# Running sums of attention weights moved half a visit later in the last two batches

## The chip, the cores and the metric

The kernel runs on one core of a Trainium2 chip. The metric is the device time of one execution in microseconds. The median of three runs of the kernel before is 1086.68 us (1086.46 to 1087.05).

## The reference, cut to what matters

Attention with hashed buckets, over 4 batches, 8 heads, 768 positions and 64 features, followed by a mixing block with a Fourier transform and a two-layer network on 512 channels:

```python
q_bucket = np.sum((q @ proj > 0) * powers, axis=-1)      # 6 bits; k_bucket alike
mask = q_bucket[:, :, :, None] == k_bucket[:, :, None, :]
scores = np.where(mask, scale * q @ k.T, -1e9)
attn = softmax(scores)                                   # numerator / (sum over keys + 1e-9)
x = (attn @ v) laid out as (B, S, H*D)

mixed = np.real(fft(fft(x, axis=1), axis=2))
u = x + mixed
un = (u - mean(u)) / sqrt(var(u) + 1e-6)
out = u + relu(un @ w_ch1) @ w_ch2
```

For this document the denominator matters: the sum over all keys of the masked exponentials. The kernel adds up the masked weights of the six chunks of keys in a tile `acc`, and sums over partitions only once for each pair of heads.

## The kernel before, in words

Work is done batch by batch. Attention of batch b runs beside the mixing block of batch b-1, which is a Python generator called `other`; between two steps of the attention generator, two or three steps of `other` are taken. For the first batch the order of instructions on each engine is as written. For the others a planner orders each engine's queue: an instruction goes out when its data and buffers are ready in the planner's own account of time, the earliest written first; scores and values (`behind`) are given precedence over what was written up to 500 instructions earlier. The order is fixed before the kernel runs, and each engine takes its queue in that order.

Attention handles a pair of heads n (n = 4b + t, four pairs in a batch) and six chunks c of 128 keys. For one chunk TensorE multiplies scores `sc` (L905) for both heads and both halves of the queries, ScalarE writes their exponentials into one of two buffers `pk` (L916), VectorE masks these in place, one instruction for each head (L930), TensorE multiplies with v into `oo` (L941), and VectorE adds the chunk's weights to `acc` (L1018, 128 partitions x 1536 elements). The first two chunks' weights are added straight out of the two buffers, so there are five sums in a pair. After the last chunk, `scale` sums `acc` over partitions with TensorE (`sum`, L960), and VectorE and ScalarE make the reciprocals (L967 to L981) and multiply x by them. `acc` has one buffer: the first sum of a pair comes after the `sum` matmuls of the pair before.

In the first two batches (n < 8) a visit handles one chunk. In the last two (n >= 8, batches 2 and 3 of 0 to 3) a visit with even c handles two chunks: scores, values of the chunk two before, exponentials, masks and sum of c, then the same of c+1. The visit with odd c does no attention work but takes a step of `prepare` (transposes L779 and hash bits of the next pair) or of `fold` (the first step of the mixing block), and then `other` goes on.

`other`, the mixing block, has four stages: matmuls `cs` (L1133); matmuls `A` and `B` (L1162), whose results VectorE adds into x (L1176); the hidden layer's products `h_p` (L1441), which ScalarE copies out of PSUM (L1463 to L1492) and VectorE combines (L1467, L1474, L1479, L1483, L1491); and the outer products `o` (L1320), which VectorE adds to the result (L1332). Hidden layer and outer products come twice in a batch. A and B, `h_p`, `o`, `sum` and the bits use one PSUM pool of two banks, so that a product can only start when VectorE or ScalarE has emptied a bank. SP issues the loads of q, k and v as well as the fetches of weights `w` (L1414, L1325).

`done_by` remembers the newest instruction on ScalarE and on VectorE of certain kinds: exponentials, masks (L930), additions into x (L1176), and most of the hidden layer's copies and additions. `in_turn()` queues what is written inside it behind these, each on its own engine. That is an order alone; it waits for no completion.

Of the kernel before, what the change touches and what calls it, by code (L numbers as in the profile page):

```python
# [485 lines left out]
def _main(  # L486
# [27 lines left out]
    def wt(shape, dtype, tag, name, bufs=2):  # L514
        return work.tile(shape, dtype, tag=tag, name=name, bufs=bufs)
# [95 lines left out]
    for i in range(NPK):  # L611
        pk = const.tile([P, 2, 2, HALF + 1], F32, tag=f"pk{i}", name=f"pk{i}")
# [70 lines left out]
    @contextmanager  # L683
    def in_turn():

        with ExitStack() as st:
            for ins in done_by.values():
                st.enter_context(tc.issue_after(ins.ins))
            yield
# [186 lines left out]
    @contextmanager  # L876
    def behind():

        with tc.issue_after(last[0].ins), tc.high_priority(offset=AHEAD):
            yield  # L880
# [3 lines left out]
    def scores(n, c, glued=False):  # L884

        qt, kt, qb, kb = preps[n]
        pss = []
        ks = slice(c * P, (c + 1) * P)
        heads = [slice(h * D, (h + 1) * D) for h in range(2)]
        for g in range(2):  # L890
            qs = slice(g * HALF, (g + 1) * HALF)
            ps = ps_sc.tile([P, 2, 512], F32, tag="sc", name=f"sc{n}_{g}_{c}")
            if kb is None:

                at = (c + (NT // 2 if g else 0)) % NT * P
                for h, rows in enumerate(heads):
                    nc.tensor.matmul(
                        ps[:, h, 0:HALF], qb[rows, 1, at : at + P],
                        qb[rows, 0, g * HALF : (g + 1) * HALF],
                        start=True, stop=False,  # L900
                    )

            for h, rows in enumerate(heads):
                with behind() if (g + h or glued) and n >= NPAIR else nullcontext():
                    last[0] = nc.tensor.matmul(  # L905
                        ps[:, h, 0:HALF], kt[rows, ks], qt[rows, qs],
                        start=kb is not None, stop=True,
                    )
            if n < TWO:
                weights(pks[npk[0] % NPK], g, ps)  # L910
            pss.append(ps)
        return pss

    def weights(pk, g, ps):

        done_by[ET.Activation] = nc.scalar.activation(  # L916
            pk[:, g, :, 0:HALF], ps[:, :, 0:HALF], AF.Exp, scale=SCALE
        )

    def weigh(n, c, pss):  # L920

        qb, kb = preps[n][2:]
        pk = pks[npk[0] % NPK]
        npk[0] += 1
        for g in range(2) if n >= TWO else ():
            weights(pk, g, pss[g])
        if kb is not None:
            for h in range(2):
                w = pk[:, :, h, 0:HALF]
                done_by[ET.DVE] = nc.vector.scalar_tensor_tensor(  # L930
                    w, qb[:, h].rearrange("p (g s) -> p g s", g=2), kb[:, h, c : c + 1], w,
                    op0=ALU.is_equal, op1=ALU.mult,
                )
        return pk

    def values(n, c, pk, oos):

        for g in range(2):
            w = HALF + 1 - g
            for h in range(2):  # L940
                oo = nc.tensor.matmul(  # L941
                    oos[g][h * D : (h + 1) * D, 0:w], nat["v", n][:, (2 * c + h) * D : (2 * c + h + 1) * D],
                    pk[:, g, h, 0:w], start=(c == 0), stop=(c == NT - 1),
                )
        last[0] = oo

    def scale(n, oos, sums):


        x = xs[n // NPAIR][:, n % NPAIR]  # L950
        vs = wt([P, 1], F32, "vs", f"vs{n}")
        nc.scalar.copy(vs, oos[0][:, HALF : HALF + 1])
        halves = [x[:, g * HALF : (g + 1) * HALF] for g in range(2)]
        for g, xg in enumerate(halves):
            nc.scalar.activation(xg, oos[g][:, 0:HALF], AF.Identity, bias=vs)

        ps = pt([P, HALF], f"sum{n}")
        for i, part in enumerate(sums):
            for j in range(4):
                nc.tensor.matmul(  # L960
                    ps[32 * j : 32 * j + 32, :], ones, part[:, j // 2, j % 2],
                    start=(i == 0), stop=(i == len(sums) - 1),
                )


        rt = wt([P, S], F32, "rt", f"rt{n}", 1)
        nc.vector.transpose(rt[:, 0:HALF], ps)  # L967
        rc = wt([P, HALF // 32], F32, "rc", f"rc{n}")
        nc.vector.tensor_scalar(rc, rt[:, 0:HALF:32], S * EPS, None, op0=ALU.add)
        nc.vector.reciprocal(rc, rc)  # L970
        yield
        rr = wt([P, 2, HALF // 32], F32, "rr", f"rr{n}")
        for g in range(2):
            for i in range(4):
                j = 2 * g + i // 2
                nc.scalar.copy(rr[32 * i : 32 * i + 32, g], rc[32 * j : 32 * j + 32])  # L976
        nc.vector.transpose(
            rt.rearrange("p (j i) -> p j i", i=32),
            rr.rearrange("p g j -> p (g j)")[:, :, None].broadcast_to([P, S // 32, 32]),
        )  # L980
        nc.vector.tensor_tensor(x, x, rt, op=ALU.mult)  # L981

    def attention(b):
        xs[b] = wt([P, NPAIR, S], F32, "x", f"x{b}")
        pending, scales = [], []

        def finish():
            n, c, pk, oos, sums = pending.pop(0)
            with behind() if n >= NPAIR and t is not None else nullcontext():
                values(n, c, pk, oos)  # L990
            if c == NT - 1:
                scales.append(scale(n, oos, sums))
                next(scales[-1])

        for t in range(NPAIR):
            n = NPAIR * b + t
            half = fold(b, 0) if t == NPAIR - 1 else iter(())
            if 1 < n + 1 < NPAIR * B:
                load(n + 1)
            ahead = prepare(n + 1) if n + 1 < NPAIR * B else iter(())  # L1000
            oos = [ps_o.tile([P, 512], F32, tag="o", name=f"oo{n}_{g}") for g in range(2)]
            acc = wt([P, 2, 2, HALF], F32, "acc", f"acc{n}", 1)
            first = None
            def chunk(c, pss):

                nonlocal first
                pk = weigh(n, c, pss)
                new = pk[:, :, :, 0:HALF]
                sums = [acc]
                if c == 0:  # L1010
                    first = new
                elif c == NT - 1 and b == 0:

                    sums.append(new)
                else:

                    for g in (0, 1) if b == 0 else (slice(0, 2),):
                        nc.vector.tensor_tensor(  # L1018
                            acc[:, g], (first if c == 1 else acc)[:, g], new[:, g],
                            op=ALU.add,  # L1020
                        )
                return n, c, pk, oos, sums

            for c in range(NT):
                if n < TWO:
                    new = chunk(c, scores(n, c))

                    for sc in scales:
                        next(sc, None)
                    scales.clear()  # L1030
                    while pending:
                        finish()
                    for sc in scales if b else ():
                        next(sc, None)
                    pending.append(new)
                elif c % 2 == 0:
                    pss = scores(n, c)
                    if len(pending) > 1:
                        finish()
                    new = [chunk(c, pss)]  # L1040
                    if pending:
                        finish()
                    new.append(chunk(c + 1, scores(n, c + 1, True)))
                    for sc in scales:
                        next(sc, None)
                    scales.clear()
                    pending += new
                if c > (3 if b == 1 else 2):
                    next(half, None)
                if c > 0:  # L1050
                    next(ahead, None)
                yield
        t = None
        while pending:
            finish()
        for sc in scales:
            next(sc, None)
# [586 lines left out]
```

## Time and profile before

| | |
|---|---|
| median of three runs | 1086.68 us |
| the profiled execution | 1086.83 us |
| its span, first to last instruction | 1085.0 us |
| TensorE busy | 1034.9 us, 95% |
| VectorE busy | 789.9 us, 73% |
| ScalarE busy | 498.4 us, 46% |
| running sums L1018, all batches | 92 instructions |
| masks L930 | 132 instructions, 128.9 us |
| granted TensorE clock | 0.995 |

Busy time is the time in which an engine executes. PE is TensorE, DVE VectorE, ACT ScalarE, SP the engine that issues most DMAs. In a line of the timeline stand the start in us from the beginning of the span, the time taken, the engine and line of code, the operation with what it writes and reads, how many were merged, and, in brackets, how long the engine had been idle before and what ended that. A line of the waits names who waited for whom, the us in total, how often, and the longest.

### The profile page before, as it was taken

The page shows a single profiled execution, that of the slowest core. Times are in us where ns is not written, and L with a number is a line of the kernel's source. Part 1 is how long each engine was busy: PE and PEld are TensorE (multiplying, and loading weights), DVE is VectorE, ACT ScalarE, POOL GpSimd, SP SyncE. Part 2 cuts the span into 40 slices and gives each one's busy share as a digit, 9 for nine tenths or more (in the row PEclk, how much of TensorE's full clock was granted, in tenths as well). Part 3 has the DMA queues.
Part 4 walks back from the last instruction along what each step waited for, and adds up shares of the span by engine and source line. Part 5 has one row for each costly group of instructions (what it writes and reads, how often), then busy time and mean ns, then how long its engine had stood idle before and what let it go on. Part 6 is the DMA issues. An engine that isn't in the chain of part 4 may idle for free.

```text
span 1085.0 us, 14130 instructions
## 1 busy us (share of the span) xinstructions
PE 1034.9 (95%) x4933; PEld 633.1 (58%) x4933; DVE 789.9 (73%) x1336; ACT 498.4 (46%) x1055; POOL 58.3 (5%) x132
## 2 busy tenths in 40 slices
PE   7989898999999999999999999999999999999997
PEld 3333364547644675545664576645675579768676
DVE  5899969887699978685948776876865875644353
ACT  6988554762277233545335424354315522340430
POOL 0000000002000020010000020001000002100000
PEclk9999999999999999999999999999999999999999
DMA  8663452380056260223062233213033205122401
GB/s 214 190 142 76 97 144 54 121 243 1 22 133 229 71 205 15 59 68 83 11 190 72 60 97 126 44 44 91 17 100 100 73 20 175 58 80 85 129 20 42
DMA packets 175710, 103.13 MB, mean 95 GB/s; under 512 B 129552, under 2 KB 162960, under 8 KB 175632
## 3 DMA queue, kind: packets, MB, share of 16 engines
q1 hardware_dynamic: 169840, 88.65, 30.3%
q0 software_dynamic: 4224, 13.11, 3.9%
q8 instruction: 41, 0.67, 0.3%
q10 hardware_dynamic: 1568, 0.39, 0.2%
q14 instruction: 37, 0.30, 0.1%
HBM read 81.14 MB, written 20.97 MB: 94 GB/s over the span
## 4 chain that ended last, share of the span: by engine, by line
PE 64%; DVE 24%; ACT 6%; issue 3%; SPq 1%; DMA 1%; DVEq 0%; ACTq 0%
PE o L1320 24%; PE h_p L1441 19%; PE oo L941 7%; PE sc L905 6%; DVE pk L930 5%; DVE acc L1018 5%; PE cs L1133 2%; PE A L1162 1%; ACT pk L916 1%; ACT rr L976 1%; PE B L1162 1%; DMA kn<-in_k_dram 1%; SPq L576 1%; DVE w L643 1%; DVE qt L779 1%
## 5 line engine op out<-in xcount | busy, mean ns | idle before, releaser
L1320 PE MATMUL o<-w,h 128*128 128x256 f32 x1152 | 258.8, 381 | 2.4 <-ACT tq L1339 0.9
L1320 PEld LDWEIGHTS o<-w,h 128*128 128x128 f32 x1152 | 216.7, 190 | 42.9 <-issue 4.3
L916 ACT ACTIVATE pk<-sc 128x768 f32<-128x768 f32 x192 | 147.3, 808 | 98.2 <-PE sc L905 32.9
L1441 PE MATMUL h_p<-x,w 128*128 128x384 f32 x448 | 162.3, 492 | 0.1
L905 PE MATMUL sc<-qt,kt 64*128 64x384 f32 x768 | 154.8, 506 | 3.6 <-ACT pk L916 3.3
L930 DVE SCALAR_TENSOR_TENSOR pk<-qb,kb,pk 128x768 f32<-128x768 bf16 x132 | 128.9, 1011 | 33.4 <-ACT pk L916 33.1
L941 PE MATMUL oo<-pk,vn 128*64 128x385 f32 (+1 forms) x768 | 148.1, 497 | 4.0 <-DVE pk L930 3.4
L1441 PEld LDWEIGHTS h_p<-x,w 128*128 128x128 f32 x448 | 82.6, 190 | 64.2 <-issue 7.7
L1018 DVE TENSOR_TENSOR acc<-acc,pk 128x1536 f32<-128x1536 f32 (+1 forms) x72 | 105.8, 1484 | 5.8 <-ACT pk L916 5.1
L1441 PE MATMUL h_p<-w 128*128 128x384 f32 x288 | 106.4, 492 | 3.5 <-ACT w L1478 2.3
L941 PEld LDWEIGHTS oo<-pk,vn 128*64 128x64 f32 x768 | 50.8, 136 | 91.6 <-issue 74.2
L905 PEld LDWEIGHTS sc<-qt,kt 64*128 64x128 f32 x768 | 66.9, 188 | 55.0 <-issue 19.3
L1441 PEld LDWEIGHTS h_p<-w 128*128 128x128 f32 x288 | 53.0, 190 | 45.5 <-ACT w L1490 5.1
L1332 DVE SCALAR_TENSOR_TENSOR w<-o,rs,w 128x256 f32<-128x256 f32 x56 | 26.7, 479 | 42.6 <-PE o L1320 42.6
L1350 ACT COPY tq<-o 128x256 f32<-128x256 f32 x24 | 8.9, 372 | 102.6 <-PE o L1320 102.6
L1320 PE MATMUL o<-w 128*128 128x256 f32 x176 | 42.1, 382 | 1.0 <-DVE w L1332 1.0
L1474 DVE TENSOR_TENSOR h<-h 128x384 f32<-128x384 f32 x32 | 17.7, 553 | 30.3 <-ACT h L1473 30.3
L1320 PEld LDWEIGHTS o<-w 128*128 128x128 f32 x176 | 33.0, 190 | 7.7 <-DVE w L1332 2.0
L1467 DVE TENSOR_TENSOR h<-h 128x384 f32<-128x384 f32 x32 | 17.7, 553 | 26.6 <-ACT h L1466 26.6
L1071 POOL DMA_DIRECT2D out_dram<-w x30 | 16.4, 548 | 368.1 <-ACT tq L1350 146.2
L1366 DVE TENSOR_TENSOR tq<-tq,o 128x256 f32<-128x256 f32 x24 | 10.0, 418 | 35.0 <-PE o L1320 35.0
L1339 ACT COPY tq<-o 128x256 f32<-128x256 f32 x24 | 8.8, 368 | 54.0 <-PE o L1320 53.9
(170 smaller groups left out, 1332.9 us busy)
## 6 DMA issues: line engine op xcount, KB each, us to landing
w<-ad SPq DMA_DIRECT2D x168, 128.0 KB, 2.0
w<-bd SPq DMA_DIRECT2D x42, 512.0 KB, 4.5
zraw<-in_moe_w_ch_dram POOLq DMA_DIRECT2D x16, 512.0 KB, 4.2
bd<-w SPq DMA_DIRECT2D x14, 512.0 KB, 3.6
vn<-in_v_dram SPq DMA_DIRECT2D x32, 192.0 KB, 3.5
qn<-in_q_dram SPq DMA_DIRECT2D x120, 48.0 KB, 2.4
kn<-in_k_dram SPq DMA_DIRECT2D x60, 96.0 KB, 3.1
zraw<-in_moe_w_ch_dram SPq DMA_DIRECT2D x8, 512.0 KB, 6.8
```

The lines of the kernel that those rows point to most:

```text
L905: last[0] = nc.tensor.matmul(ps[:, h, 0:HALF], kt[rows, ks], qt[rows, qs], start=kb is not None, stop=True,)
L916: done_by[ET.Activation] = nc.scalar.activation(pk[:, g, :, 0:HALF], ps[:, :, 0:HALF], AF.Exp, scale=SCALE)
L930: done_by[ET.DVE] = nc.vector.scalar_tensor_tensor(w, qb[:, h].rearrange("p (g s) -> p g s", g=2), kb[:, h, c : c + 1], w, op0=ALU.is_equa ...
L941: oo = nc.tensor.matmul(oos[g][h * D : (h + 1) * D, 0:w], nat["v", n][:, (2 * c + h) * D : (2 * c + h + 1) * D], pk[:, g, h, 0:w], start=( ...
L1018: nc.vector.tensor_tensor(acc[:, g], (first if c == 1 else acc)[:, g], new[:, g], op=ALU.add,)
L1133: nc.tensor.matmul(ps[:, pc + 2 * lo : pc + 2 * hi - 1 : 2], z[:, cp, pc, par, t * P : (t + 1) * P], ch[:, cp, pc, lo:hi], start=(cp == 0) ...
L1162: nc.tensor.matmul(ps[:, cols], F[:, par, k, t, j * P : (j + 1) * P], sq[:, t, k, cols], start=(t == 0), stop=(t == 1),)
L1320: nc.tensor.matmul(ps, a[:, r], right7[i][:, r], start=start and r == 0, stop=r == HF // 2 - 1, skip_group_check=not start,)
L1332: nc.vector.scalar_tensor_tensor(t[:, cols], src, r, t[:, cols], op0=ALU.mult, op1=ALU.add)
L1441: nc.tensor.matmul(ps, left[:, k], right[i][:, k], start=start and k == 0, stop=k == 1, skip_group_check=not start,)
L1467: done_by[ET.DVE] = nc.vector.tensor_tensor(c21, c12, c21, op=ALU.add)
L1474: done_by[ET.DVE] = nc.vector.tensor_tensor(c22, c21, c22, op=ALU.add)
```

## The change

In the two-chunk batches the running sums of both chunks of a visit are no longer written directly behind each chunk's masks, but in the following visit with odd c, which so far did nothing in `attention` but its steps of `fold` and `prepare`. They are written inside `in_turn()`, and so are queued on VectorE behind the newest instruction in `done_by`: a mask, an addition into x, or an addition of the hidden layer. `chunk` keeps scores' exponentials and masks; the sums are a function `tally` of their own. In the one-chunk batches `tally` follows `chunk` at once, as before.

```diff
             def chunk(c, pss):
 
+                return n, c, weigh(n, c, pss), oos, [acc]
+
+            def tally(c, pk, sums):
+
                 nonlocal first
-                pk = weigh(n, c, pss)
                 new = pk[:, :, :, 0:HALF]
-                sums = [acc]
                 if c == 0:
                     first = new
                 elif c == NT - 1 and b == 0:
...
                             acc[:, g], (first if c == 1 else acc)[:, g], new[:, g],
                             op=ALU.add,
                         )
-                return n, c, pk, oos, sums
 
             for c in range(NT):
                 if n < TWO:
                     new = chunk(c, scores(n, c))
+                    tally(c, new[2], new[4])
...
                     pending += new
+                else:
+                    with in_turn():
+                        for p in pending:
+                            tally(p[1], p[2], p[4])
                 if c > (3 if b == 1 else 2):
                     next(half, None)
```

## Prediction

> **What bounds the kernel now.** I read the page's first parts, then the waits of TensorE in the stretch of each of the last two batches of attention, and then the timeline of VectorE where the longest of those waits lies. The page:
>
> ```profile
> span 1085.0 us, 14130 instructions
> PE 1034.9 (95%) x4933; PEld 633.1 (58%) x4933; DVE 789.9 (73%) x1336; ACT 498.4 (46%) x1055; POOL 58.3 (5%) x132
> PEclk9999999999999999999999999999999999999999
> L1018 DVE TENSOR_TENSOR acc<-acc,pk 128x1536 f32<-128x1536 f32 (+1 forms) x72 | 105.8, 1484 | 5.8 <-ACT pk L916 5.1
> ```
>
> TensorE is the bound and its clock is full, so a gain can only come out of the time in which it waits. The running sums, L1018, are VectorE work. Asked for that line from 395 to 890 us, the trace shows 40 of the large form, 32 acc<-acc,pk and 8 acc<-pk,pk, of 1752 and 1738 ns: the sums of the two batches that are changed, 20 in each, 70 us of VectorE. The third batch's attention lies from about 397 to 655 us, the fourth's from 655 to 890. What TensorE waited for from 395 to 655 us (total us, times, longest):
>
> ```profile
> PE A L1162 <- DVE x L1176: 2.1, 2, 1.6
> PE h_p L1441 <- ACT w L1478: 1.1, 1, 1.1
> PE o L1320 <- DVE w L1332: 0.8, 2, 0.6
> PE oo L941 <- DVE pk L930: 0.7, 1, 0.7
> PE bits L836 <- ACT h L1466: 0.6, 1, 0.6
> PE h_p L1441 <- ACT w L1490: 0.6, 1, 0.6
> ```
>
> From 655 to 890 us the answer is the same but for bits, which is gone, and o, which is 0.3. So everything that a better order on VectorE can give back is 5.9 us in the third batch and 4.8 in the fourth (2.1 + 1.1 + 0.3 + 0.7 + 0.6), 10.7 us in all, 1% of the span. Now the order on VectorE at the longest wait:
>
> ```profile
> 418.76 1.95 DVE L930 SCALAR_TENSOR_TENSOR pk<-qb,kb,pk 128x768 f32<-128x768 bf16 x2 [1.46 <-ACT pk L916]
> 420.74 1.76 DVE L1018 TENSOR_TENSOR acc<-acc,pk 128x1536 f32<-128x1536 f32 x1
> 422.42 0.97 DVE L779 STREAM_TRANSPOSE qt<-qn 128x768 f32<-128x768 f32 x1
> 423.31 1.90 DVE L930 SCALAR_TENSOR_TENSOR pk<-qb,kb,pk 128x768 f32<-128x768 bf16 x2
> 425.14 1.01 DVE L1176 TENSOR_TENSOR x<-x,A 128x384 f32<-128x384 f32 x2
> 426.06 1.01 DVE L1176 TENSOR_TENSOR x<-x,B 128x384 f32<-128x384 f32 x2
> 427.00 1.75 DVE L1018 TENSOR_TENSOR acc<-acc,pk 128x1536 f32<-128x1536 f32 x1
> 428.66 1.01 DVE L1176 TENSOR_TENSOR x<-x,A 128x384 f32<-128x384 f32 x2
> ```
>
> The chain is: running sum, mask, addition into x, and only that addition frees the PSUM bank for the next A. TensorE's own row there:
>
> ```profile
> 426.29 1.54 PE L1162 MATMUL A<-sq,F 128*128 128x193 f32 x8 [1.56 <-DVE x L1176]
> ```
>
> The second sum, at 427.00, holds the next addition back until 428.66, and A waits again, 0.51 us at 429.82.
>
> **What the Trainium skill says.** "PSUM — Partial Sum Buffer", section Engine vs sequencer instructions: "ScalarE/VectorE/GpSimdE queues are strict FIFO." The timeline agrees: the additions into x stand behind the sums and the mask although the first A had been multiplied by about 423. "VectorE: DVE Perf Modes", section The TRN2 errata, gives an fp32 addition of two tensors as (N + 151)/0.96 ns, 1757 ns for N = 1536; the trace has 1752, and 1.67 from one start to the next (a sum at 525.10, the mask behind it at 526.77 us). "Perfetto Trace Analysis", section Identifying the Most-Contended Engine, warns that matmul busy time is no measure of closeness to the roofline; here I therefore use TensorE's waits and not its 5% idle.
>
> **The change part by part.** (1) Removed: nothing. The same 40 sums run, 0 us of VectorE saved. No matmul, activation or DMA is added. (2) Moved: in each of the 24 two-chunk visits the sum no longer stands between the mask of chunk c and that of c+1. The second mask can come up to 1.67 us sooner, where its exponential is done by then (at 534 it is not: exponentials end at 536.55, and the mask starts at 538.38 behind a sum and a transpose, so 1.8 us). (3) Added: an order, not a semaphore. The pair of sums (one in a pair's first visit) follows the newest mask, addition into x, or addition L1467, L1474, L1483 or L1491 of the hidden layer, whichever was issued last in the program. Each pair is one block of 3.4 us. Queued behind it on VectorE: the operand sums L1419 to L1426, L1305 and L1306, the transposes L779 of the next heads, and the next visit's masks. Through the data, the next exponentials into the two pk buffers wait for it, and TensorE's scores behind those. On SP, loads of q and k wait for L779 (76.6 and 20.3 us of SP waiting in 395 to 890), and the fetches of w stand behind these; the transposes are filled into VectorE's gaps early already (422.42), so I put SP's share at nothing; with a transpose 3.4 us later and no fetch in stock it would cost up to 3.4 at one place.
>
> Now the waits one at a time. A on x: without the sum at 420.74, transpose and mask end at about 423.5 instead of 425.2, A's bank is free 1.65 us sooner, and 1.56 goes. Without the one at 427.00 the 0.51 goes. h_p on w L1478, 1.13 us at 458.80: ScalarE had first to do the eight small copies of rr, 456.59 to 458.25, which waited for rc L969 at 455.77, behind the sum at 454.13 to 455.85; 1.7 us sooner, and the 1.13 goes. o on w L1332, 0.57 at 543.26 in the third batch: the addition stood behind a sum at 541.10; it goes. In the fourth batch, 0.34 at 876.36 behind the sum at 874.16 goes likewise. bits, 0.60 at 601.58: ScalarE waited for L1483, which stood behind the sum at 597.72; it goes. Sum: third batch 1.56 + 0.51 + 1.13 + 0.57 + 0.60 = 4.37; fourth 1.56 + 0.51 + 1.13 + 0.34 = 3.54; together 7.9 us. The oo wait on a mask (0.69) and the h_p wait on L1490 (0.57) I leave as they are, replaced by others of their kind: between none and both of them go, 0 to 2.5 us.
>
> New cost at the passage from A and B to the hidden layer. The two sums of a pair's last visit now follow the fourth addition into x, and L1420, which makes an operand of the second product, comes behind them: 3.4 us from the end of L1176 to its start, and 0.95 for itself, about 4.4; with the last B's 1.0 of evacuation, 5.5 us in which TensorE cannot have that product. Cover: un, 12 matmuls at 0.11, 1.3 us; two other products of two matmuls each, four at 0.33 (10.52 us for 32 at 558.68), 1.3; the scores of the next pair's second chunk, 1.5. That is 4.1, so 1.4 us of wait, twice 2.8. Bounds: 0 if the values (2.74 us) are issued there too; 2.9 each if the scores are late, since their bank needs an exponential that itself waits for the sum. At the passage to the outer products (500 us) the same block falls on L1305 to L1340 and L1332; there scores and values, 1.49 + 2.74, cover its 3.4 us, and I count nothing; uncovered it would be 2.6 each.
>
> In the hidden layer's stages exponentials now wait for a sum that waits for an addition of `other`. Some four visits in each batch lie there. Nothing of that order is in the trace. I bound each at 0 to 0.57 (the L1490 wait), below nothing too since the masks come earlier there, down to -0.3, and take a quarter, 8 x 0.14 = 1.1. In the outer products' stages only the order of two operations on VectorE changes, under a TensorE that runs without a gap (o in 216 ns each): nothing.
>
> Sum: -7.9 + 2.8 + 1.1 = -4.0 us. The profiled execution took 1086.83 us (span 1085.0 and 1.8 around it), 0.15 above the median of 1086.68, so 1082.8 against its own time and 1082.7 against the median.
>
> **The rivals.** *Held buffers (slower).* There are two pk buffers, and a sum half a visit later holds both. For: exponentials already waited for a sum four times, 4.1 us; so far they could run ahead of the hidden layer (scores of the second pair's last visit at 467.95, with the layer at its second column block), and that lead is taken away. Price: 2.9 at each A passage, 5.8, and 0.69 (the oo wait) at each of the eight visits, 5.5: 11.3 - 7.9 = +3.4, 1090.1 us. It decides once new waits are above 7.9 us, a third of a us per visit. Against: the other batch's products run gapless alone (h_p 28 in 9.61 us at 485.5), and TensorE's order is planned with them as a filling. *No difference.* The planner fills every gap from what is ready, and the waits move to other places: 1086.7. For: it moved even transposes of the pair after next forward. Against: waits at A are caused by data and banks, and have nothing else to fill them. *More than forecast.* Nothing new appears and all 10.7 us go: 1076. For: the 7.4 us bursts of mask, sum, mask, sum on VectorE become two of under 4. Against: the block of 3.4 at the A passage.
>
> **How the numbers follow.** A measurement of this kernel tells about 0.2%, 2.2 us, from no change. The forecast's case (2 to 6.5 us faster) has 0.40, more than forecast 0.16, no difference 0.13, slower 0.31. So faster 0.56, same 0.13, slower 0.31. With both signs likely, the likeliest case's own range is 1080.0 to 1084.5; the range for eight in ten goes from 1077.0 (nearly all waits gone) to 1091.0 (the held buffers, at a little over their price).
>
> **What would show it.** The waits of A on x at the two passages gone, and no sum between a mask and an addition L1176; the wait of h_p on L1478 after rr gone; 40 sums of 1.75 us still. Wrong: a wait of un, h_p or sc of over 1.5 us just after the last A, TensorE's waits on pk or L1420; exponentials that wait for L1018 for much more than 4.1 us; SP's fetches of w behind later transposes. A gain of another size with these waits gone would mean that the order on TensorE itself changed, which my sum takes as kept.

## The result, and the profile after

The changed kernel takes 1081.10 us (median of 6 runs, 1080.72 to 1082.37) where the kernel before takes 1086.57; the ratio is 0.9952, 95% interval 0.9941 to 0.9962. It is faster by about half a per cent: 5.2 us by the ratio, 5.5 between the medians. A later group of runs gave 0.9948 (0.9935 to 0.9962).

The page of the changed kernel has the same work in a shorter span. Line numbers move by two at the sums (L1018 is L1020), and by six behind them (L1162 is L1168, L1176 is L1182, L1441 is L1447).

```profile
span 1080.1 us, 14131 instructions
PE 1036.7 (96%) x4933; PEld 633.0 (59%) x4933; DVE 789.2 (73%) x1336; ACT 500.4 (46%) x1055; POOL 59.1 (5%) x132
L1020 DVE TENSOR_TENSOR acc<-acc,pk 128x1536 f32<-128x1536 f32 (+1 forms) x72 | 106.0, 1485 | 5.3 <-ACT pk L916 5.1
```

There are as many matmuls and as many VectorE instructions as before, and the sums take as long. What TensorE waited for in the changed kernel from 395 to 655 us (us in total, times, longest):

```profile
PE A L1168 <- DVE x L1182: 1.2, 2, 0.7
PE un L1194 <- DVE x L1182: 0.7, 1, 0.7
PE sc L905 <- ACT pk L916: 0.3, 1, 0.3
PE un L1194 <- ACT w L1195: 0.2, 1, 0.2
PE h_p L1447 <- DVE rt L967: 0.2, 1, 0.2
```

From 655 to 890 us the answer is the same. The waits come to 2.6 us in each batch, where before they were 6.4 (the six lines shown with the prediction and two small ones) and 5.3. So 6.5 us of listed waiting went.

The stage that the change touches can be cut out of the trace: it runs from the first `cs` matmul of the third batch's attention to that of the mixing block behind the fourth's. It began at 401.71 and ended at 911.48 us before, and at 402.35 and 906.45 after: 509.77 against 504.10 us, 5.67 less. In the second profile of the changed kernel it is 504.06. This length repeats far better than the span, whose first 400 us, with the same work in all, differ by up to 2.5 us from one profiled execution to the next (the last section shows what goes with that); I use it below beside the ratios, and call it the stage.

At the passage where A waited longest, VectorE's order and A's own row are now:

```profile
419.40 1.95 DVE L930 SCALAR_TENSOR_TENSOR pk<-qb,kb,pk 128x768 f32<-128x768 bf16 x2 [0.80 <-ACT pk L916]
421.26 0.97 DVE L779 STREAM_TRANSPOSE qt<-qn 128x768 f32<-128x768 f32 x1
422.16 1.95 DVE L930 SCALAR_TENSOR_TENSOR pk<-qb,kb,pk 128x768 f32<-128x768 bf16 x2
424.02 0.97 DVE L779 STREAM_TRANSPOSE kt<-kn 128x768 f32<-128x768 f32 x1
424.92 0.98 DVE L1182 TENSOR_TENSOR x<-x,A 128x384 f32<-128x384 f32 x2
425.82 1.01 DVE L1182 TENSOR_TENSOR x<-x,B 128x384 f32<-128x384 f32 x2
426.04 1.54 PE L1168 MATMUL A<-sq,F 128*128 128x193 f32 x8 [0.68 <-DVE x L1182]
```

The sum between the masks is gone. But half of what it left was filled by the planner: a second transpose, for a pair two ahead, has moved in front of the addition into x. A still waits, 0.68 instead of 1.56 us. The two sums stand behind the fourth addition into x, with one of the operand sums between them:

```profile
439.92 1.02 DVE L1182 TENSOR_TENSOR x<-x,B 128x384 f32<-128x384 f32 x2 [0.28 <-PE B L1168]
440.86 1.75 DVE L1020 TENSOR_TENSOR acc<-acc,pk 128x1536 f32<-128x1536 f32 x1
442.53 0.95 DVE L1426 TENSOR_TENSOR w<-x,w 128x768 f32<-128x768 f32 x1
443.39 1.75 DVE L1020 TENSOR_TENSOR acc<-acc,pk 128x1536 f32<-128x1536 f32 x1
```

### The profile page after: what moved, and what is told of

It reads as the page before. It is cut to its first block, busy times and chain, and to the rows that moved or that the text cites. A ratio compares the mean times of both kernels' runs of the same rounds, so it can differ in the third digit from the quotient of the medians.

```text
span 1080.1 us, 14131 instructions
## 1 busy us (share of the span) xinstructions
PE 1036.7 (96%) x4933; PEld 633.0 (59%) x4933; DVE 789.2 (73%) x1336; ACT 500.4 (46%) x1055; POOL 59.1 (5%) x132
## 4 chain that ended last, share of the span: by engine, by line
PE 71%; DVE 17%; ACT 6%; issue 3%; SPq 2%; DMA 1%; DVEq 0%; ACTq 0%
PE o L1326 26%; PE h_p L1447 21%; PE oo L941 8%; PE sc L905 8%; DVE acc L1020 3%; DVE pk L930 3%; PE cs L1139 2%; PE A L1168 2%; ACT pk L916 2%; PE B L1168 1%; SPq L576 1%; DMA kn<-in_k_dram 1%; ACT rr L976 1%; DVE x L1182 1%; DVE w L643 1%
## 5 line engine op out<-in xcount | busy, mean ns | idle before, releaser
L1447 PE MATMUL h_p<-x,w 128*128 128x384 f32 x448 | 164.1, 494 | 0.8 <-DVE rt L967 0.4
L1447 PEld LDWEIGHTS h_p<-x,w 128*128 128x128 f32 x448 | 82.0, 190 | 66.7 <-issue 9.9
L1020 DVE TENSOR_TENSOR acc<-acc,pk 128x1536 f32<-128x1536 f32 (+1 forms) x72 | 106.0, 1485 | 5.3 <-ACT pk L916 5.1
L1447 PE MATMUL h_p<-w 128*128 128x384 f32 x288 | 106.1, 490 | 0.1
L1447 PEld LDWEIGHTS h_p<-w 128*128 128x128 f32 x288 | 53.6, 190 | 39.6 <-ACT w L1484 2.4
```

The lines of the kernel that those rows point to most:

```text
L1020: nc.vector.tensor_tensor(acc[:, g], (first if c == 1 else acc)[:, g], new[:, g], op=ALU.add,)
L1447: nc.tensor.matmul(ps, left[:, k], right[i][:, k], start=start and k == 0, stop=k == 1, skip_group_check=not start,)
```

## The experiments

There were twelve runs: ten kernels, and two of the kernels once more. Each was timed at least five times, beside the kernel before on the same chip. Ratios are to that, with their 95% intervals; stages are of one profiled execution each.

My theory was that TensorE lost its time behind sums which stood on VectorE in front of additions that free a PSUM bank or let ScalarE go on, and that the queue behind the newest addition takes them out of the way. Rivals: moving them is enough without the queue; the earlier second mask is what counts; attention that no longer runs ahead is what counts; VectorE's load as such is what counts.

**Moved, but not queued**

```diff
-                    with in_turn():
-                        for p in pending:
-                            tally(p[1], p[2], p[4])
+                    for p in pending:
+                        tally(p[1], p[2], p[4])
```

> The sums half a visit later as in the changed kernel, but without the order behind the newest mask or addition. Theory (VectorE's order): the planner sends a sum out as soon as it is ready and VectorE has nothing earlier; at the A passage and in the hidden layer's stages the sums come back in front of additions that are not yet ready, so a part of the gain is lost: 1082.5 to 1085. Rival (being written half a visit later is enough): as the changed kernel, 1081.1 within 0.5.

Measured: 1088.70 us, ratio 1.0022 (1.0015 to 1.0030), stage 512.17. It is slower than the kernel before, so both expectations missed: I had thought that part of the gain would stay. TensorE's waits from 395 to 890 us, its four longest (lines are five further down than before here):

```profile
PE A L1167 <- DVE x L1181: 3.1, 2, 1.6
PE h_p L1446 <- ACT w L1495: 2.7, 4, 1.0
PE sc L905 <- ACT pk L916: 2.5, 4, 1.0
PE h_p L1446 <- ACT w L1483: 2.3, 2, 1.1
```

A's long wait and the waits of h_p on ScalarE's copies are there again, and scores wait for exponentials, 2.5 us instead of 0.6. Written later, a sum is ready at once, and the planner sends it out as soon as VectorE is free in its account. At 419.00 us a sum stands between the two masks in front of the additions into x again, as at 420.74 before. The queue is what makes the change a gain.

**Both sums behind both masks, in the same visit**

```diff
                     pending += new
-                else:
-                    with in_turn():
-                        for p in pending:
-                            tally(p[1], p[2], p[4])
+                    for p in new:
+                        tally(p[1], p[2], p[4])
```

> Both sums of a visit in the same visit, behind both masks, not half a visit later and behind no addition. Theory: the sums still stand in front of the additions into x and of the hidden layer, so most of the waits of TensorE stay: 1084.5 to 1086.5. Rival (the gain is the second mask's earlier start): 1081 to 1082.5, and the wait of oo on a mask is gone.

Measured: 1086.42 us, ratio 0.9999 (0.9991 to 1.0008), stage 509.74 against 509.77. As the theory had it. The wait of oo on a mask is gone, as the rival said, and others have come up to its worth, among them (lines are four further down than before)

```profile
PE A L1166 <- DVE x L1180: 4.2, 4, 1.6
PE sc L905 <- ACT pk L916: 2.5, 4, 1.0
PE h_p L1445 <- ACT w L1482: 2.3, 2, 1.1
```

The wait of oo was dearer than its 0.69 us in the list. Here a row of 16 oo matmuls runs through; in the kernel before the mask broke it in two (the first line is of this run, the other two of the kernel before):

```profile
463.06 2.81 PE L941 MATMUL oo<-pk,vn 128*64 128x385 f32 x16
463.67 2.15 PE L941 MATMUL oo<-pk,vn 128*64 128x385 f32 x10
466.51 1.51 PE L941 MATMUL oo<-pk,vn 128*64 128x385 f32 x6 [0.69 <-DVE pk L930]
```

From 463.67 to 468.02 that is 4.35 us instead of 2.81: 1.54 lost, once in each batch, so 3.1 us in all. The other waits grew by 3.0 (listed from 395 to 890 us, 13.3 here; 11.7 before, of which 1.4 were on oo). So an earlier second mask alone is worth nothing: what it gives at oo, later waits take back.

**What the sums cost at all**

```diff
-                else:
+                elif n >= TWO:
+                    if c == 1:
+                        nc.vector.scalar_tensor_tensor(
+                            acc, first, 1.0, new, op0=ALU.add, op1=ALU.add
+                        )
+                else:
```

The kernel before, without 32 of the 40 sums: 56 us of VectorE less.

> The kernel before, with only the first of the five sums of a pair in the two-chunk batches (it adds 1, so that no sum is zero); the other 32 sums of 1.75 us are left out, which makes the denominators wrong. It bounds what the sums cost at all. Theory: the sums cost what TensorE waited behind them, so 1079.5 to 1081.5, little better than the changed kernel with all 40 sums. Rival (VectorE's load itself bounds a stage): clearly below, 1072 to 1078.

Measured: 1079.47 us, ratio 0.9939 (0.9926 to 0.9953), stage 503.57. In the stage the 32 sums had cost 6.2 us; with all of them in place the changed kernel has 504.10, 0.5 more than without them. By the stage the change took over nine tenths of what these sums cost (5.67 of 6.2), by the ratios, which spread more, about eight tenths (0.48 of 0.61%). VectorE's 56 us in themselves bound nothing. The planner orders this kernel anew too, so 6.2 us is a measure and not a strict bound.

**Attention held back in another way**

```diff
-            weights(pk, g, pss[g])
+            with in_turn() if g == 0 else nullcontext():
+                weights(pk, g, pss[g])
```

The kernel before, its sums in place; ScalarE's exponentials are queued behind the newest of the other work's copies.

> The kernel before, sums in their old place, but each chunk's exponentials queued on ScalarE behind the newest copy of the other's work, so that attention may not run ahead of the hidden layer, as in the changed kernel. Theory (VectorE's order): no gain or a loss, 1085.5 to 1089, since the sums still stand in front of additions. Rival (the gain comes from attention no longer running ahead, which changes TensorE's order): 1081 to 1083.5.

Measured: 1093.97 us, ratio 1.0073 (1.0059 to 1.0087), stage 517.15. The rival falls for this way of holding attention back: it does not help, it costs 7.4 us of the stage, more than I had expected. The waits listed for TensorE, 10.6 us, are even a little shorter than before (11.7); what grew is how often TensorE goes from one kind of product to another, 212 times in the stage instead of 180. Two h_p matmuls in a row start 0.323 us apart, an h_p and a score matmul behind it 0.416. There were 21 such steps instead of 6. Four rows of 16 oo matmuls also took 0.9 us longer each than an unbroken one (at 453.56, 479.25, 715.74 and 741.42 us), with less than 0.1 of it showing as a wait; before, two such rows took 1.54 longer. I did not settle how much of the 7.4 us is due to which.

**One part of the pairs at a time**

```diff
-                else:
+                elif t == 0:          # or t == 1, t > 1, t < 2
                     with in_turn():
...
+                if n >= TWO and not (t == 0):
+                    tally(c, new[2], new[4])
```

In the pairs that are left out the sums stand right behind each mask, as before.

> The change in the first pair of heads of each two-chunk batch alone (beside the stages cs, A and B); in the other pairs the sums stand right behind each mask as before. By the prediction's steps: A's 2.07 us go and up to 1.4 come at the passage, in each of two batches, so 1.3 us faster than before, 1085. If the gain is made elsewhere: no difference.

> The change in the second pair alone (beside the first half of the hidden layer). By the waits of the kernel before: h_p on the copy L1478 1.13, oo on a mask 0.69 and h_p on L1490 0.57 go, in two batches 4.8 us at most, of which the prediction counted 2.3 and charged 1.1: between 1081.5 and 1085. If attention held back costs there: slower than before.

> The change in the third and fourth pairs alone (beside the outer products, the second half of the hidden layer and the second outer products). By the prediction's steps: o on L1332 0.57 and 0.34 and bits 0.60 go, 1.5 us, 1084.8. If these waits only move: no difference.

| the change in | median us | ratio | stage, us against before |
|---|---|---|---|
| first pair | 1092.05 | 1.0048 (1.0035 to 1.0061) | +4.5 |
| second pair | 1086.22 | 0.9999 (0.9991 to 1.0007) | +0.2 |
| third and fourth | 1084.57 | 0.9981 (0.9974 to 0.9987) | -2.3 |
| sum of the three | | | +2.4 |
| all, the changed kernel | 1081.10 | 0.9952 (0.9941 to 0.9962) | -5.7 |

The last pairs came out as expected. The first two did not: the first pair alone is a loss where I expected 1.3 us of gain, and the second alone is worth nothing, where I expected 1.5 to 5 us. With the second pair alone the waits of h_p and oo that I had named are gone, but `un` waits 1.5 us for ScalarE's copy L1491, and three kinds of wait in the third pair, 2.2 us, are new (shown with the next test). Parts that add up to a loss make a gain together. With the first pair alone TensorE waits 3.48 us at one place in each batch. The timeline there (here L1476 is the addition L1467 of before, L1483 is L1474, L1488 is L1479, and L1491 the copy L1482):

```profile
473.77 0.55 DVE L1476 TENSOR_TENSOR h<-h 128x384 f32<-128x384 f32 x1
474.24 1.75 DVE L1023 TENSOR_TENSOR acc<-acc,pk 128x1536 f32<-128x1536 f32 x1
475.91 0.97 DVE L779 STREAM_TRANSPOSE kt<-kn 128x768 f32<-128x768 f32 x1
476.81 0.51 DVE L1483 TENSOR_TENSOR h<-h 128x384 f32<-128x384 f32 x1
477.42 0.56 DVE L1488 TENSOR_TENSOR h<-h,w 128x384 f32<-128x384 f32 x1
478.01 0.52 ACT L1489 ACTIVATE h<-h 128x384 f32<-128x384 f32 x1 [4.60 <-DVE h L1488]
478.44 0.46 ACT L1491 COPY h<-h_p 128x384 f32<-128x384 f32 x1
478.96 2.08 PE L1450 MATMUL h_p<-x,w 128*128 128x384 f32 x4 [3.48 <-ACT h L1491]
```

A sum of the second pair, unqueued, stands with a transpose in front of the hidden layer's additions. ScalarE waits 4.60 us for L1488 with a ReLU, and the copy that would free TensorE's bank is behind that ReLU. The first pair's change had worked up to there: the h_p matmuls that start at 469.44 before start at 466.18, 2.3 us earlier counted from the start of each stage. With this other timing a sum of the second pair meets the hidden layer's additions in this place; queued behind them, it could not stand in front. TensorE's clock fell after each of the two waits, which by the last section's reckoning makes 3.4 of the 4.5 us. That suggested a test of the two together.

> The change in the first and the second pair of each two-chunk batch together; the third and fourth as before. Alone, the first pair was 0.48% slower and the second made no difference, and the third and fourth alone were 0.19% faster. Theory now (the first pair's delay pushes the second pair's sums in front of the hidden layer's additions, and only queueing these too takes the harm away): 1083.2 to 1084.5, the gain of the whole less that of the last pairs. If the parts simply add up: 1091 to 1092.

Measured: 1087.09 us, ratio 0.9994 (0.9985 to 1.0003), stage 509.19, 0.6 less than before. This misses the expected range: the second pair's queue does take the first pair's harm away (5.1 us of the stage), but the gain of 3 us isn't there. The waits up to 500 us are those of the changed kernel; from the third pair on there are new ones, the first of them behind an unqueued sum and a mask (from 395 to 890 us):

```profile
PE o L1329 <- DVE tq L1375: 1.0, 2, 0.5
PE qb L850 <- ACT pk L916: 0.7, 2, 0.3
PE kb L860 <- DVE qb L535: 0.5, 2, 0.3
```

The changed kernel has none of these three, and the second pair alone has the same three: they come where the second pair is queued and the third is not. So a pair's queue also guards against what the earlier pairs' new timing does to it. But the waits are not the whole account: listed, they come to 8.9 us, 2.8 less than before, while the stage is only 0.6 shorter. The other 2.2 us lie in TensorE's time between the listed waits, and their cause stays open.

**Queued behind masks and additions into x alone**

```diff
-                    with in_turn():
+                    with tc.issue_after(newest[0].ins):   # newest mask or L1176
```

> The changed kernel, but the sums are queued only behind the newest mask or addition into x, not behind the hidden layer's additions L1467, L1474, L1483 and L1491. Theory now (in the hidden layer's stages a sum in front of an addition is what costs): the second pair's sums stand in front of these again, as with the first pair alone: slower than before, 1087 to 1092. Rival (the order at the passage of A and B is what counts): as the changed kernel, 1081 to 1082.

Measured: 1083.87 us, ratio 0.9975 (0.9964 to 0.9985), stage 506.44. Neither: it keeps 3.3 of the 5.7 us. Its longest wait is in the hidden layer, behind two sums that stand in front of its additions, and is much shorter than with the first pair alone (1.4 against 3.5 us at its longest):

```profile
PE h_p L1448 <- ACT w L1497: 2.5, 2, 1.4
```

**Transposes queued too**

```diff
-                nc.vector.transpose(to, at)
+                with in_turn() if n > TWO else nullcontext():
+                    nc.vector.transpose(to, at)
```

> The changed kernel, and the transposes of q and k of later pairs queued in the same way behind the newest mask or addition. In the changed kernel a transpose of k at 424.02 stands between the mask and the first addition into x, and A still waits 0.68 us at 426.04. Theory (VectorE's order at the A passage): this wait goes in both batches, 1.4 us, 1079.7 against 1081.1. Against: the loads of q and k, which wait for these transposes on SP, come later, and the fetches of w behind them: not faster, up to 1085.

> The changed kernel once more, on the same chip as the others of this group: 1081.1 within 1, ratio 0.995.

> The changed kernel with the transposes of later pairs queued too, once more, beside the changed kernel on the same chip. If the 1.2 us that its span was shorter come from its order (A's wait was 1.1 instead of 2.5): 0.8 to 1.5 us below the changed kernel here. If it was the state of the chip: equal within 0.3.

Measured: 1080.23 us, ratio 0.9940 (0.9927 to 0.9953); in the later group 1080.28, 0.9941 (0.9927 to 0.9954), beside 1080.71, 0.9948 (0.9935 to 0.9962), for the changed kernel again. A's waits fall from 2.5 to 1.1 us as the theory had it, but the stage is 503.88 and 503.87 us, only 0.2 below the changed kernel's. The medians lie 0.4 us apart on one chip, between what the two expectations said, and the intervals overlap, so I claim no better kernel; most of the 1.4 us that went came back elsewhere, in part as a new 0.6 of h_p on ScalarE.

## Why the prediction was right, and where not

The direction and the size were right: -4.0 forecast, about -5.2 measured, inside the likeliest case. The mechanism was right in the main: sums on VectorE in front of additions and copies that TensorE needs. That the size fits is in part luck. As the list of waits has it, the sum credited 2.3 us too much at A, left 2.5 uncredited at oo and h_p, and charged 2.1 too much for new waits; these errors, 2.3 one way and 4.6 the other, half cancelled. Point by point:

- *The ceiling.* 10.7 us of waits was put as all that could come back; 6.5 went. Leaving 32 of the sums out gave 6.2 us of the stage, nearer to what came, and the list of waits did not show it. Nor is the list a ceiling: the two oo waits stand in it with 1.4 us and cost 3.1.
- *A on x.* Put at -2.07 in each batch, measured -0.9 (2.1 to 1.2). The sum did leave; the planner filled half of its place with a transpose, and a later A waits 0.55 for the addition before it. The gain here came to less than half of what was put. The planner's filling was my rival "no difference", and at this one place it held in part.
- *h_p on L1478, o on L1332, bits.* Put at -1.13, -0.57, -0.34, -0.60: all gone.
- *oo on a mask and h_p on L1490.* Left as they were, with 0 to 2.5 us of gain as bounds; both gone, 1.26 in each batch as listed, and 2.1 with the whole of the broken oo row. Taking the lower end was the largest step that made the sum too small. The run with both sums behind both masks shows why caution had a ground: there the oo wait went and others took its place.
- *The passage to the hidden layer.* Charged 1.4 in each batch for a late L1420. A wait of 0.7 is there, on `un`, but it is for the fourth addition into x and not for the operand sums: the planner put L1426 between the two sums, and the block of 3.4 us that I had reckoned with never formed there.
- *The hidden layer's stages.* Charged 1.1 for exponentials held back; h_p waits 0.2 for rt in each batch, and nothing for exponentials. *Held buffers*, the slower rival: ScalarE waited for the sums four times before, 4.1 us, and not once after. It falls. Whether attention's lead is in itself worth something stays open: held back by another queue the kernel lost 7.4 us, but with more changes of kind on TensorE and other rows of oo broken.
- *Kept order on TensorE.* The sum took it as kept; it changed. TensorE goes from kind to kind 196 times instead of 180 in the stage, and the stage became shorter by 5.67 us while 6.5 us of listed waits went and the two unbroken oo rows gave 1.7 more. So about 2.5 us came back in TensorE's time between waits. That the changes of kind are what cost them was not measured by itself.
- *That waits are independent terms.* This silent step was wrong. By it the first pair alone would gain 1.3 us, and it loses 4.5; the parts come to +2.4, and the whole to -5.7. Of these 4.5, 3.4 are the clock's (last section), for which the sum had no term. The total came out near because all pairs were changed together.

## What to carry to other kernels

Work that nobody waits for soon must not only be written later; it needs a place in the queue behind what others wait for, since a planner sends it out the moment it is ready (moved alone: 0.2% slower; moved and queued: 0.5% faster). Before predicting such a reordering, price the moved work by leaving it out, which here came near to the gain directly (6.2 us of stage for 32 sums, 5.7 gained), and don't add up gains of single waits: a shift in one stage moves later work into new collisions. Here the first two pairs paid only with the later ones queued too; the last two paid by themselves.

## What the runs showed of the hardware

After the 3.48 us of waiting with the first pair alone, TensorE ran at half its clock for a while. Busy time and granted clock by stretch (us, then each engine's busy us, the clock as PEclk):

```profile
475.00:479.00 4.00, 0.52 (x3) 0.04 (x1) 2.94 (x5) 0.89 (x2) 0.00 (x0) 1.00 0.75 185
479.00:481.00 2.00, 2.00 (x5) 1.09 (x6) 1.04 (x2) 0.89 (x2) 0.00 (x0) 0.72 0.00 0
481.00:483.00 2.00, 2.00 (x5) 1.09 (x4) 0.01 (x1) 0.90 (x2) 0.00 (x0) 0.50 0.41 89
483.00:486.00 3.00, 3.00 (x9) 1.41 (x8) 0.56 (x1) 0.97 (x2) 0.00 (x0) 0.95 0.34 71
```

In these rows the clock is the third figure from the end: 0.72 and then 0.50 just after the wait, 0.95 from 483 us on. Six starts of h_p came 0.16 to 0.32 us late each, 1.7 us in all, so the wait cost half as much again. It happened in both batches: 3.4 us of the stage.

The Trainium skill, "TensorE: Matmul & The Clock Gate", section What's actually happening, says that the clock falls to half after an idle window of about 3.4 us; this wait, 3.48 us, is just over that. But in this case shorter waits went before a fall too. Ahead of the stage, in the kernel before and in the run that was moved but not queued, TensorE waits at the same place for nearly the same time; the clock then falls in the one and not in the other (the first two lines are of the kernel before):

```profile
75.92 0.34 PE L897 MATMUL sc<-qkb 64*128 64x384 bf16 x2 [1.98 <-ACT pk L916]
77.00:79.00 2.00, 2.00 (x10) 0.92 (x8) 2.00 (x3) 1.22 (x4) 0.00 (x0) 0.50 0.68 115
75.26 0.34 PE L897 MATMUL sc<-qkb 64*128 64x384 bf16 x2 [1.96 <-ACT pk L916]
77.00:79.00 2.00, 2.00 (x18) 0.62 (x16) 2.00 (x3) 2.00 (x5) 0.00 (x0) 1.00 0.48 79
```

So the measurements here do not give 3.4 us of waiting as a safe limit, and a wait of 2 us goes before a fall in one execution and not in another; what decides it stays open. The waits of A, up to 1.57 us, left the clock whole (1.00 from 424 to 433 us before). Of the fourteen profiles, ten show a fall ahead of the stage, at about 76 or 117 us or at both; their stages begin at 400.87 to 402.35 us, those of the other four at 399.90 to 400.77. The changed kernel's two profiles are one of each, 402.35 and 400.52. In the stage itself the clock of the kernel before was whole (1.00 from 395 to 890 us). The row of clocks on the page can hide such falls: its slices are 27 us long, and it is 9 throughout for the kernel before and for the first pair alone.
